# Attention and feed-forward kernel on one core: w_in's split moved from ScalarE and VectorE to VectorE and GpSimd, constant products at the start, a new order

## The chip, the core and the metric

The kernel runs on one core of one Trainium2 chip. The core has a matrix engine (TensorE, PE in the profile), three engines that work on rows of data (VectorE, DVE; ScalarE, ACT; GpSimd, POOL) and a queue engine that only starts transfers (SyncE, SP). Every engine works through its own list of instructions in order. SBUF is the working memory of 128 partitions; PSUM is the small memory that products are added up in. The metric is the device time of one execution in microseconds.

## What is computed

Eight batches of twelve heads of attention over 448 positions of 64 values, where the softmax is replaced by a sigmoid, and behind it a feed-forward layer whose activation is ELU. Heads are put side by side, so that a token has 768 values.

```python
# q, k, v: (8, 12, 448, 64); w_in: (768, 2048); w_out: (2048, 768)
scores = scale * np.matmul(q, k.transpose(0, 1, 3, 2)) - np.log(S)
attn = 1.0 / (1.0 + np.exp(-scores))
attn_out = np.matmul(attn, v)
x = attn_out.transpose(0, 2, 1, 3).reshape(B * S, H * D)
h = x @ w_in
g = np.where(h > 0.0, h, np.exp(np.minimum(h, 0.0)) - 1.0)
out = g @ w_out
```

## The kernel before

**Precision.** The products run in 16-bit floats, but the result is to have more than 16 bits give. So each operand is scaled by a power of two and split into a high part (the value rounded to f16) and a low part (the value minus its high part, in f16), and each product is made of three: high by high, high by low, low by high. For w_in and w_out that split is preceded by a reading of 64-bit words from the two matrices, which are taken apart, and by the search for the scale. The first six of the 48 pairs of heads are multiplied in f32 instead (`EXACT`).

**Stages.** A pair of heads goes through loads, maxima, scales, split, transposes, scores (`Pair.scores`, `psc`), sigmoid (`soften`, `sg`), its own split, and the product with v (`Pair.values`, `pav`), which gives rows of `xh`. A layer b then goes through the 16 columns blocks f of w_in (`Expert.products`, tile `ph`), exponential, missing part, ELU (`e`), the split into `g`, and the second product with w_out (`moe2_tile`, `po`).

**What sets the order.** Everything up to the start of layer 1 is written out by hand in the string `ORDER`: 890 letters, each of which takes one step of a generator (the dictionary `streams` names them). A step issues its instructions on whatever engines it uses, so the string sets the order on every engine at once; there is no scheduler behind it (`manual_schedule`). From layer 1 on the order is that of a plain loop over layers, with `fill` putting pieces of `moe2` between pieces of attention.

**How w_in gets ready** (letters i, A to G; 16 steps each, one for a block of 768 by 128 values). The letter i loads a block's words. A takes the magnitudes' upper field (`field`) and its last bits (`last_bits`), two instructions of ScalarE, into one of five staging places in `g` (`staged(f)`). B puts them together on VectorE (`magnitudes`). C adds up the magnitudes by six products with a constant (`si`). D takes the greatest sum on VectorE and makes the scale `ws`, the last instruction of it on GpSimd (`twice_inverse`). E puts the signs back, in place, on VectorE (`signed`). F makes the high part: ScalarE multiplies the staged f32 block by the scale and writes f16 (`w_in_high`, L291). G makes the low part: VectorE multiplies the staged block by the scale and subtracts the high part (`w_in_low`, helper `low`, L189). A staging place is free for block f+5 when G of block f has read it.

**How a pair of the first six gets turned** (letters d, e). TensorE transposes q and k into PSUM (`transposes`, tile `pt`), and VectorE copies the 896 columns into SBUF (`copied`, L492).

The lines of the steps of w_in on which the change works:

```python
# w_in_high
nc.scalar.mul(wi[:, 0, :, f * P : (f + 1) * P], staged(f), w_in_scale[f])
# w_in_low
d = wi[:, :, :, f * P : (f + 1) * P]
low(d[:, 1], staged(f), w_in_scale.pop(f), d[:, 0])
# twice_inverse, the last instruction of a scale
nc.gpsimd.tensor_scalar(dst, dst, 2 / least, None, op0=ALU.min)
```

Other letters that matter below: m is `Expert.products` of layer 0, R the rescaling of layer 0's `xh` to one scale (`rescale`, five multiplications on VectorE and then `greatest`, whose tile is `dg`); it needs the scales of all six pairs, which GpSimd carries on from pair to pair (`value_scale`, tile `xs`). The letter p is a piece of the second product, H to N are for w_out what A to G are for w_in.

Of the kernel before, what the change touches and what calls it, by code (L numbers as in the profile page):

```python
# [11 lines left out]
F32 = mybir.dt.float32  # L12
# [4 lines left out]
ALU = mybir.AluOpType  # L17
# [14 lines left out]


ORDER = (
    "iqviqviiiAAAadbceSTABCDEaSTFdbWBceCSSWDEAABGTTFCWWEGDAABSCiqvXFAATATAiiYYDGBECEaSSBFWbCD"
    "TTAAFAAdWWWcEDeGBGSCBSCEEqivFTXATASTiiiiqAAYDaWdbDGBYceWWCSSFFBDGEAATTTCBDEWCSSXAATTFEYD"
    "GWvBaYiiqdWCbWWGceFAAAADEBGSSCBDTFTAXAvadCbSToHEceSSYGRERYRDBRRiTHTAAWWWWCSTBIXFYSCEYEDR"
    "WTWTWWooHHqHvaRIauXHoHHFoHHqvYYIRRJJrJKKRDIsoKombJaaKxlHmoycbxHlffHHfsIcGsIygggsInHHIzGm"
    "JJmJJxlzyxzlLwyMMNNKmmmxFMMKNNKlzMMxlNyzMNwGyKtuoqvoffxMHlfHzHHmmgaNxMlaIgywNbJKyINMFzxm"
    "xMFlloNMHHJKowcwwwyygImmtzxHHlJNGKIyzxzzlfmffxMlqoHHJmwGwKyNywINvmzxzMlxMlfJwKwwgNymzxag"  # L40
    "ygaNzloHHMywINSSppppppppppTzJKwwgqovtpppppppppppppppppppkHHTIJKojSSbppppppppppppppppcaTT"
    "fffTHHaggIkJLMMNMNNMMNNMNgSSpbpWpppWpWppWTMMTNNKMMNNXYfgtqjvMMSSTNNcMYNMNffMgNMNkappWpWW"
    "WfppSTXTUgagVppppSSppfTTUUTpppppbUgYVqtvjkSSWcYVTTfUpWSpWpVaapppbppWpTfUUgVgSSppfUfXVVVg"
    "YcgkYWWTTUUSWWpptqvjSTSXRRVRRYVUVYRpWppTTTUUVSWWWaVSpppppppTXUTUfUffYYRVRVVgaWWWWppppfXY"
    "Ygggkjqjtv"
)


# [1 line left out]
def attention_ffn(  # L50
# [9 lines left out]
    nc = tc.nc  # L60
    B, H, S, D = q.shape
    DM, DF = w_in.shape
    P = 128
# [13 lines left out]
    WHOLE = FIRST + 2  # L77
    SP = 4
    SKEW = 2
    assert 2 * D == P and 2 * R == P and NK == NP  # L80

    const = ctx.enter_context(tc.tile_pool(name="const", bufs=1))
    sb = ctx.enter_context(tc.tile_pool(name="sb", bufs=1))
    ps = ctx.enter_context(tc.tile_pool(name="ps", bufs=1, space=PSUM))
# [7 lines left out]
    wi = const.tile([P, 2, NK, DF], F16, name="wi")  # L92
# [24 lines left out]
    w_in_words = []  # L117
    ones = const.tile([P, P], BF16, name="ones")
    nc.vector.memset(ones, 1.0)
    w_ones = const.tile([P, P], BF16, name="w_ones")  # L120
    nc.gpsimd.memset(w_ones, 2.0 ** (1 - WTOP))
    x_ones = const.tile([P, P], BF16, name="x_ones")
# [65 lines left out]
    def low(lo, src, s, hi):  # L188
        nc.vector.scalar_tensor_tensor(lo, src, s, hi, op0=ALU.mult, op1=ALU.subtract)  # L189
# [53 lines left out]
    def staged(f):  # L243
        return stage[:, (f + WT - NF) % WT].rearrange("p (c x) -> p c x", c=NK)
# [10 lines left out]
    w_in_sums, w_in_scale = {}, {}  # L255
# [32 lines left out]

    def w_in_high():
        for f in range(NF):  # L290
            nc.scalar.mul(wi[:, 0, :, f * P : (f + 1) * P], staged(f), w_in_scale[f])  # L291
            yield

    def w_in_low():
        for f in range(NF):
            d = wi[:, :, :, f * P : (f + 1) * P]
            low(d[:, 1], staged(f), w_in_scale.pop(f), d[:, 0])
            yield
    def w_in_ratios():
        nc.vector.tensor_reduce(wm[:, 0:1], wp, axis=AX.X, op=ALU.max)  # L300
# [30 lines left out]
    def w_out_fields():  # L331
        for i, f in each_w_out(NW):
            if f < NW - 1:
                t = wo[:, i, 2 * f + SKEW : 2 * f + SKEW + 2].rearrange("p f j c -> p f (j c)")
                t = t.bitcast(F32)
# [96 lines left out]
    class Preparation:  # L432
# [56 lines left out]

        def copied(self):  # L490
            qk = early[:, self.hp % 2]
            nc.vector.tensor_copy(qk, self.pt[:, : 2 * S])  # L492
            ready[self.n] = self.x_scale, 1 / math.sqrt(D), [qk], [self.rv]

        def natural(self, i):
# [606 lines left out]
    def outputs():  # L1102
# [6 lines left out]
        "t": pair_turned(), "u": whole_values(), "j": outputs(),  # L1109
        "A": w_in_fields(), "B": w_in_magnitudes(), "C": w_in_add(), "D": w_in_scales(),  # L1110
        "E": w_in_signs(), "F": w_in_high(), "G": w_in_low(),
        "H": w_out_fields(), "I": w_out_magnitudes(), "J": w_out_add(), "K": w_out_signs(),
        "L": w_out_scales(), "M": w_out_high(), "N": w_out_low(),
# [128 lines left out]
```

## Time and profile before

| | |
|---|---|
| three runs | 1170.59, 1171.21 and 1177.94 us, median 1171.21 us |
| the profiled execution | 1176.26 us, of which 1174.4 us are its span |
| mean granted TensorE clock | 0.993 of full speed |
| busy: PE, DVE, ACT, POOL | 1144.0, 728.6, 797.2, 182.4 us |
| chain that ended last | PE 85% of the span |

The span runs from the first instruction to the last; the 1.9 us around it belong to the execution's time. The profiled execution is 5.05 us (0.4%) above the median of the runs. A PE that is busy is not a PE at its peak, since matmuls overlap and their ends are modelled; what the table does show is that the other engines have room over the span as a whole. It says nothing of a stage, and the change lies in the first stage alone.

In the profile's views a row names a line of the kernel, an engine, an operation, the tiles (out<-in), the partitions by the elements of each, and how often. L189 is the helper `low`, L148 the last line of `twice_inverse`.

### The profile page before, as it was taken

Reading aid. Unit: us, or ns where it says so; the run is one execution under the profiler, and the core shown is the slowest. Engines: PE = TensorE matmul, PEld = TensorE weight load, DVE = VectorE, ACT = ScalarE, POOL = GpSimd, SP = SyncE. Lnnn points to the kernel's source line nnn. Section 1 sums busy time; section 2 is a strip of 40 time slices with the busy share of each in tenths; the row PEclk is TensorE's granted clock in tenths of the full one; section 3 lists DMA queues with packets and bytes.
Section 4 is the critical chain, followed back from the end, with each engine's and each line's share of the span. In section 5 each row is a group of like instructions: output and inputs, shape, how many; then the busy total and the mean of one; then the engine's idle time right before and its main releaser. Section 6 shows DMA issues by size and latency. Waiting matters only on the chain.

```text
span 1174.4 us, 23748 instructions
## 1 busy us (share of the span) xinstructions
PE 1144.0 (97%) x9662; PEld 635.1 (54%) x9662; DVE 728.6 (62%) x1346; ACT 797.2 (68%) x1184; POOL 182.4 (16%) x502
## 2 busy tenths in 40 slices
PE   5989899999999999999999999999999999999998
PEld 2335465555666555555666555555566555655565
DVE  5999868955666557855566556765476564853300
ACT  6989859777665678856766568857766567856500
POOL 2224113111121002201121111301022000300000
PEclk9999999999999999999999999999999999999999
DMA  9996544231242122503054131621234121310000
GB/s 261 254 259 181 123 127 95 58 85 41 55 102 62 41 41 58 125 24 80 8 103 102 24 66 28 122 55 42 48 73 94 45 51 38 72 37 1 1 27 27
DMA packets 219038, 92.12 MB, mean 78 GB/s; under 512 B 182448, under 2 KB 214832, under 8 KB 218928
## 3 DMA queue, kind: packets, MB, share of 16 engines
q1 hardware_dynamic: 217856, 90.28, 32.6%
q8 instruction: 75, 1.23, 0.4%
q10 hardware_dynamic: 1072, 0.33, 0.1%
q14 instruction: 35, 0.29, 0.1%
HBM read 60.29 MB, written 11.01 MB: 61 GB/s over the span
## 4 chain that ended last, share of the span: by engine, by line
PE 85%; ACT 2%; DVE 1%; DMA 1%; issue 0%; SPq 0%; POOL 0%; DVEq 0%; ACTq 0%; POOLq 0%
PE ph L728 33%; PE po L794 31%; PE pav L620 7%; PE psc L551 6%; PE po_r L794 5%; PE pscr L651 1%; DMA rv<-in_v_dram 1%; DMA ats<-in_moe_w_out_dram 1%; ACT wo L372 0%; DVE wo L189 0%; ACT wo L205 0%; ACT g L757 0%; ACT e L745 0%; ACT ats L210 0%; PE so L223 0%
## 5 line engine op out<-in xcount | busy, mean ns | idle before, releaser
L728 PE MATMUL ph<-xh,wi 128*128 128x448 f16 x2304 | 440.9, 353 | 0.4 <-DVE e L751 0.4
L794 PE MATMUL po<-wo,g 128*64 128x384 f16 (+1 forms) x4320 | 394.0, 327 | 0.0
L794 PEld LDWEIGHTS <-g 128*64 128x64 f16 (+1 forms) x4992 | 290.0, 109 | 161.7 <-issue 32.5
L728 PEld LDWEIGHTS <-wi 128*128 128x128 f16 x2304 | 224.0, 98 | 211.0 <-issue 5.0
L751 DVE SCALAR_TENSOR_TENSOR e<-ph,e 128x448 f32<-128x448 f32 x128 | 79.7, 623 | 183.7 <-ACT e L745 183.6
L189 DVE SCALAR_TENSOR_TENSOR ats<-sg,ats 128x896 f16<-128x896 f32 x120 | 127.6, 1089 | 104.4 <-ACT ats L588 104.4
L738 ACT ACTIVATE e<-ph,msc 128x448 f32<-128x448 f32 x128 | 80.7, 631 | 112.1 <-PE ph L728 94.5
L558 ACT ACTIVATE sg<-psc,bias,sc 128x896 f32<-128x896 f32 x126 | 134.1, 1094 | 6.4 <-PE psc L551 3.2
L627 ACT ACTIVATE xh<-pav,sc 128x448 f16<-128x448 f32 x48 | 30.4, 633 | 121.4 <-PE pav L620 119.7
L588 ACT ACTIVATE ats<-sg 128x896 f16<-128x896 f32 x120 | 109.5, 947 | 0.8 <-PE pav L620 0.2
L745 ACT ACTIVATE e<-e,msc 128x448 f32<-128x448 f32 x128 | 97.1, 760 | 4.3
L757 ACT ACTIVATE g<-e,rr 128x384 f16<-128x384 f32 (+1 forms) x192 | 95.3, 529 | 1.1 <-DVE e L751 0.7
L189 DVE SCALAR_TENSOR_TENSOR g<-e,rr,g 128x384 f16<-128x384 f32 (+1 forms) x192 | 94.7, 524 | 0.4
L551 PE MATMUL psc<-qk 64*128 64x448 f16 x756 | 87.0, 354 | 0.0
L148 POOL TENSOR_SCALAR sc<-sc 128x3 f32<-128x3 f32 (+1 forms) x48 | 13.5, 281 | 461.1 <-DVE pw L181 460.2
L620 PE MATMUL pav<-ats,vn 128*64 128x448 f16 x720 | 75.5, 353 | 0.0
L620 PEld LDWEIGHTS <-vn 128*64 128x64 f16 x880 | 49.8, 110 | 32.9 <-issue 2.6
L794 PE MATMUL po_r<-wo,g 128*64 128x384 f16 (+1 forms) x672 | 64.9, 326 | 0.0
L189 DVE SCALAR_TENSOR_TENSOR nat<-raw,sc,nat 128x384 f16<-128x384 f32 (+1 forms) x126 | 60.2, 525 | 1.1 <-ACT nat L503 0.3
L503 ACT ACTIVATE nat<-raw,sc 128x384 f16<-128x384 f32 (+1 forms) x126 | 59.8, 531 | 0.8 <-POOL sc L467 0.3
L189 DVE SCALAR_TENSOR_TENSOR xh<-pav,sc,xh 128x448 f16<-128x448 f32 x48 | 32.6, 680 | 39.9 <-ACT xh L627 39.9
L551 PEld LDWEIGHTS <-qk 64*128 64x128 f16 x756 | 30.2, 95 | 48.3 <-issue 29.7
(128 smaller groups left out, 968.9 us busy)
## 6 DMA issues: line engine op xcount, KB each, us to landing
wo<-in_moe_w_in_dram SPq DMA_DIRECT2D x14, 768.0 KB, 6.4
raw<-in_q_dram SPq DMA_DIRECT2D x48, 192.0 KB, 3.8
rv<-in_v_dram SPq DMA_DIRECT2D x48, 192.0 KB, 2.9
raw<-in_k_dram SPq DMA_DIRECT2D x47, 192.0 KB, 3.3
out_dram<-room SPq DMA_DIRECT2D x47, 192.0 KB, 2.1
wo<-in_moe_w_out_dram SPq DMA_DIRECT2D x9, 768.0 KB, 4.8
ats<-in_moe_w_out_dram SPq DMA_DIRECT2D x6, 768.0 KB, 4.7
rv<-in_v_dram SPq DMA_DIRECT2D x96, 32.0 KB, 2.5
```

What stands on the lines that cost most here:

```text
L189: nc.vector.scalar_tensor_tensor(lo, src, s, hi, op0=ALU.mult, op1=ALU.subtract)
L503: nc.scalar.mul(self.nat[:, 0, t : t + n], src, s)
L551: nc.tensor.matmul(psc[:, j, :S], kk[rows[j], o], qq[rows[j], :S], start=(n == 0), stop=(n == len(parts) - 1),)
L558: nc.scalar.activation(to, psc, AF.Sigmoid, bias=bias, scale=self.s_scale)
L588: nc.scalar.mul(hi, sg, 2.0**ATOP)
L620: nc.tensor.matmul(pav[rows[j], :S], vv[i][:, 2 * NC + j if g == NC else j * NC + g], sg[k][:, j], start=(g == 0 and n == 0), stop=(g == N ...
L728: nc.tensor.matmul(self.ph[f], wi[:, wj, c, f * P : (f + 1) * P], self.xh[c][:, xj], start=(n == 0), stop=(n == 3 * NK - 1),)
L738: nc.scalar.activation(self.e[f], self.ph[f], AF.Exp, scale=self.m[:, 0, f : f + 1])
L745: nc.scalar.activation(e, e, AF.Relu, bias=self.m[:, 1, f : f + 1], scale=self.m[:, 2, f : f + 1])
L751: nc.vector.scalar_tensor_tensor(e, self.ph.pop(f), 0.0, e, op0=ALU.max, op1=ALU.subtract)
L757: nc.scalar.mul(g[:, 0, f, o : o + n], self.e[f][:, i : i + n], self.xr)
L794: nc.tensor.matmul(po[r, :HM], tokens[:, r], wo[:, i, f, wj], start=(n == 0), stop=(n == 3 * NF - 1),)
```

## The change

Four things change.

1. TensorE gets 72 products of a constant matrix with itself (`ones`), 128 by 128, at the head of its list. Nothing reads their result.
2. For each of w_in's 16 blocks, F is now a multiplication of the staged f32 block by its scale, in place, on VectorE, and G is two instructions of GpSimd: a cast of the staged block to f16 (the high part) and a subtraction of that from the staged block (the low part). ScalarE's multiplication and VectorE's multiply-and-subtract are gone.
3. The copies of the six turned pairs go from VectorE to ScalarE.
4. `ORDER` is a new string of the same 890 letters, each as often as before.

```diff
-    "iqviqviiiAAAadbceSTABCDEaSTFdbWBceCSSWDEAABGTTFCWWEGDAABSCiqvXFAATATAiiYYDGBECEaSSBFWbCD"
+    "iqviiqviiAABadbCDEceSiSAABFCDEFaiTTAWAdSbcBeWSCTAATAATGAAWDBCEFWSSBEBGGTXTAAiAACCSEYDDDF"
...
+    IDLE = 72
...
     nc.vector.memset(ones, 1.0)
+    idle = ps.tile([P, 512], F32, tag="pav", name="idle")
+    for _ in range(IDLE):
+        nc.tensor.matmul(idle[:, :P], ones, ones, start=True, stop=True)
...
     def w_in_high():
         for f in range(NF):
-            nc.scalar.mul(wi[:, 0, :, f * P : (f + 1) * P], staged(f), w_in_scale[f])
+            t = staged(f)
+            nc.vector.tensor_scalar(t, t, w_in_scale[f], None, op0=ALU.mult)
             yield
 
     def w_in_low():
         for f in range(NF):
             d = wi[:, :, :, f * P : (f + 1) * P]
-            low(d[:, 1], staged(f), w_in_scale.pop(f), d[:, 0])
+            nc.gpsimd.tensor_copy(d[:, 0], staged(f))
+            nc.gpsimd.tensor_tensor(d[:, 1], staged(f), d[:, 0], op=ALU.subtract)
             yield
...
         def copied(self):
             qk = early[:, self.hp % 2]
-            nc.vector.tensor_copy(qk, self.pt[:, : 2 * S])
+            nc.scalar.copy(qk, self.pt[:, : 2 * S])
```

What the new string does to the lists of the engines is shown at three places. The first is GpSimd's list from the first pairs' scales on. Here `ws` is the scale of a block of w_in, `sc0_2`, `pw0_2` and `xs0` belong to pair 2 of layer 0, `wi` holds the split of w_in, and `g` is where its blocks are staged. Before:

```order
L423 TENSOR_SCALAR sc0_1_189<-xs0_141 128x1
L148 TENSOR_SCALAR ws_74<-ws_74 128x1 x4
L148 TENSOR_SCALAR sc0_2_348<-sc0_2_348 128x1
L184 TENSOR_SCALAR pw0_2_347<-pw0_2_347 128x1
L417 TENSOR_SCALAR xs0_141<-xs0_141,pw0_2_347 128x1
```

And now:

```order
L424 TENSOR_SCALAR xs0_226<-xs0_226,sc0_1_282 128x1
L429 TENSOR_SCALAR sc0_1_282<-xs0_226 128x1
L302 CAST wi_68<-g_70 128x6x128
L303 TENSOR_TENSOR wi_68<-g_70,wi_68 128x6x128
L152 TENSOR_SCALAR ws_74<-ws_74 128x1
```

GpSimd's list held only instructions on one column here; now the scale of block 2 (the L152) stands behind the cast and subtraction of block 0; two more pairs of cast and subtraction, of blocks 1 and 2, follow it, and only then the scales of blocks 3 to 5. Before, the scales of four blocks stood together (x4). Of the 16 casts and subtractions, 13 stand ahead of the scales of pair 5, which the rescaling of layer 0 needs; that is the second place, GpSimd's list ahead of them:

```order
L302 CAST wi_68<-g_70 128x6x128
L303 TENSOR_TENSOR wi_68<-g_70,wi_68 128x6x128
L152 TENSOR_SCALAR sc0_5_773<-sc0_5_773 128x1
L188 TENSOR_SCALAR pw0_5_772<-pw0_5_772 128x1
L423 TENSOR_SCALAR xs0_226<-xs0_226,pw0_5_772 128x1
```

Before, the same place held the scales of two blocks and no work on a block:

```order
L148 TENSOR_SCALAR ws_74<-ws_74 128x1 x2
L148 TENSOR_SCALAR sc0_5_662<-sc0_5_662 128x1
L184 TENSOR_SCALAR pw0_5_661<-pw0_5_661 128x1
L417 TENSOR_SCALAR xs0_141<-xs0_141,pw0_5_661 128x1
L418 TENSOR_SCALAR xs0_141<-xs0_141,sc0_5_662 128x1
```

What moved there is that the chain of scales from pair to pair runs behind the work on w_in. The third place is VectorE's list at the start. Before, behind three constants:

```order
L196 TENSOR_REDUCE mx0_0_121<-rv0_93 128x4
L178 TENSOR_REDUCE al_135<-pr_131 128x1
L144 TENSOR_SCALAR sc0_0_134<-al_135 128x1
L181 TENSOR_SCALAR pw0_0_133<-al_135 128x1
L492 COPY g_70<-pt0_0_123 128x896
L214 SCALAR_TENSOR_TENSOR g_70<-g_70,wo_69 128x768
```

And now:

```order
L218 SCALAR_TENSOR_TENSOR g_70<-g_70,wo_69 128x768
L200 TENSOR_REDUCE mx0_0_194<-rv0_166 128x4
L283 TENSOR_REDUCE alw_213<-si0_206 128x1
L148 TENSOR_SCALAR ws_74<-alw_213 128x1
L234 SCALAR_TENSOR_TENSOR g_70<-wo_69,g_70 128x768
L182 TENSOR_REDUCE al_220<-pr_204 128x1
```

The magnitudes of w_in's block 0 (L214, now L218) moved from behind pair 0's maxima, scales and copy to the head of the list, and the copy is gone from it. On SyncE's list the load of a third block of w_in moved ahead of q of pair 1; the loads ahead of that are the same. From layer 1 on no instruction moved.

More of the change, by code (lines that the diff above doesn't have):

```diff
@@ L34 @@
 ORDER = (
-    "iqviqviiiAAAadbceSTABCDEaSTFdbWBceCSSWDEAABGTTFCWWEGDAABSCiqvXFAATATAiiYYDGBECEaSSBFWbCD"
[L36 to L45, printed above, removed]
+    "iqviiqviiAABadbCDEceSiSAABFCDEFaiTTAWAdSbcBeWSCTAATAATGAAWDBCEFWSSBEBGGTXTAAiAACCSEYDDDF"
+    "BEFBFqiviWWTGGGAAadCqiWWCbEBDYDEceSSCAXTATYvBDFaEYFiiiqGGdWSCWbceASTABDAWCTWSATAXTSEDFEB"
+    "YFYCESGGATTAAvioiqBFaDBWdWWWbCceSCDEFDFSvGGGAHXTATSTYBEaWdWbCcYEeAHqoSSTTHWHWIITXARRYRBo"
+    "voSSTTHHHHCDaREYRRaIIWWWWXbcDYRYRJJJJKKRrRqoHHfffsIKvaKsgasgFoooougGmJmmxHlHxyIlyqtvHHHH"
+    "xlbJKKsIInymJJcLzxlzzMfMffmxKNywKalMHNgNMmmMzxHggyFNwNmMxllMNauozyzHMNbyINxMHlzMwNcFItqm"
+    "JxlfmKwNywwwMMzNfgyJKgvoHHxlMommzIwyaNzxflHxHMlJKoyGGmmNwaMzxNIyHlHxMJwNyImxlzzlJKKwwyyz"
+    "zwwwmxloHHfbcgIppppppppppJKyztNwgfffSSoqpppppppppppppppkjvHHTTgggIJKaoppppppppabpppppppH"
+    "HkISSJLTTTMMNNMNMNMNMMNNMMNMcNNppppppppWWWpSWSTMXMSKNMfTTqjtNYgNMkNfffgggvMMpppppWWWWSSf"
+    "TXTUUNYagaVNYYVjqvtppppppSSbpppTTTUUWpSSWTTUpppcaaVVVpWSppppWpppkfUTffSSpbpUUXfVgggVVTTY"
+    "gcWWWWppSjtSqvpppppUUffXTTUTUSSYRRRVRgYYVagRVkVaTTpWWWWUUSpppppXTUfUfVVYYVVpWWWpWXppppgR"
+    "RgYYktqjjv"
 )
```

## The prediction

> **What bounds the kernel now.** I read first the busy rows of the page, then the three stretches that the change divides the span into, then what TensorE waits for.
>
> ```profile
> PE 1144.0 (97%) x9662; PEld 635.1 (54%) x9662; DVE 728.6 (62%) x1346; ACT 797.2 (68%) x1184; POOL 182.4 (16%) x502
> 0.00:84.47 84.47, 63.24 (x343) 26.49 (x344) 69.59 (x134) 67.20 (x84) 19.99 (x55) 0.94 0.95 260
> 84.47:231.50 147.03, 141.32 (x1168) 75.38 (x1166) 123.38 (x222) 123.89 (x187) 38.62 (x84) 0.98 0.51 121
> 231.50:1174.40 942.90, 939.42 (x8154) 533.22 (x8153) 535.60 (x992) 606.11 (x914) 123.75 (x363) 1.00 0.25 55
> PE pt L485 <- DMA raw<-in_q_dram: 7.6, 1, 7.6
> PE si L223 <- DVE g L214: 5.2, 6, 3.1
> PE so L223 <- DVE wo L214: 3.0, 2, 2.8
> PE psc L551 <- DVE g L492: 2.0, 2, 1.5
> ```
>
> In the rows of stretches the columns behind the length are PE, weight loads, DVE, ACT and POOL, then granted clock, DMA share and GB/s. The cuts are the first matmul of layer 0 (84.47) and of layer 1 (231.50). Behind 231.50 no instruction moves, so 942.90 us stay. Between the cuts PE is busy for 141.32 of 147.03 us. In front of 84.47 it is idle for 21.2 us: there it waits, mostly for DVE. So the question is when the first matmul of layer 0 can run, and then whether PE stays as full as it was.
>
> It runs when the rescaling is through, whose last step is `dg` on DVE. DVE's groups between its first real instruction (8.97) and `dg`, by shape, those that the change touches or the sum uses, and `dg` itself from the timeline:
>
> ```profile
> L214 DVE SCALAR_TENSOR_TENSOR g<-g,wo 128x768 uint32<-128x768 uint32 x14 | 13.3, 952 | 0.0
> L230 DVE SCALAR_TENSOR_TENSOR g<-wo,g 128x768 uint32<-128x768 uint32 x14 | 13.2, 951 | 0.1
> L189 DVE SCALAR_TENSOR_TENSOR wi<-g,ws,wi 128x768 f16<-128x768 f32 x11 | 11.1, 1009 | 0.0
> L492 DVE COPY g<-pt 128x896 f32<-128x896 f32 x6 | 6.5, 1080 | 0.0
> L279 DVE TENSOR_REDUCE alw<-si 128x1 f32<-128x128 f32 x15 | 4.2, 283 | 1.8 <-PE si L223 1.8
> L144 DVE TENSOR_SCALAR ws<-alw 128x1 uint32<-128x1 uint32 x15 | 2.3, 154 | 0.5
> L674 DVE TENSOR_SCALAR xh<-xh,rr 128x896 f16<-128x896 f16 x5 | 2.1, 446 | 0.0
> L214 DVE SCALAR_TENSOR_TENSOR g<-g 128x768 uint32<-128x768 uint32 x2 | 1.9, 954 | 0.2 <-ACT g L210 0.2
> L230 DVE SCALAR_TENSOR_TENSOR g<-g 128x768 uint32<-128x768 uint32 x2 | 1.9, 953 | 0.0
> L214 DVE SCALAR_TENSOR_TENSOR wo<-wo 128x768 uint32<-128x768 uint32 x2 | 1.9, 953 | 0.0
> L214 DVE SCALAR_TENSOR_TENSOR wo<-wo,g 128x768 uint32<-128x768 uint32 x1 | 0.9, 949 | 0.0
> ...
> 83.74 0.29 DVE L153 TENSOR_SCALAR dg<-ident,rr 128x128 bf16<-128x128 f32 x1
> ```
>
> The idle column is near nothing: DVE is what bounds this stage. The change takes work from it, and gives work to POOL, busy for 19.99 of 84.47 us.
>
> **The change part by part, in this stage.**
>
> *VectorE.* Eleven L189 on wi (11.1 us) and six copies L492 (6.5) leave, 17.6 us. In come 13 multiplications in place, one more L214 (0.95), one more L279 (0.28) and four one-column instructions like L144 (0.6), as the order counts them ahead of `dg`. The in-place multiplication, one input of 768 f32, has no row. It lies between L674 (446 ns for 896 f16) and L189 (1009 ns for 768 with two inputs). I take 0.61, for L674 does 896 elements in less than half the time of L189's 768, so one-input work in SBUF is fast, and f32 has twice its bytes: 13 x 0.61 = 7.9 us (ends 5.8 and 13.1). DVE's sum falls by 17.6 - 9.7 = 7.9 us (10.0 to 2.7).
>
> *The start.*
>
> ```profile
> 6.37 0.86 ACT L210 ACTIVATE wo<-wo 128x768 uint32<-128x768 uint16 x1
> 8.97 0.69 DVE L196 TENSOR_REDUCE mx<-rv 128x4 bf16<-128x512 f32 x1 [7.76 <-DMA rv<-in_v_dram]
> 7.62 1.73 PE L485 MATMUL pt<-ident,raw 128*128 128x128 f32 x7 [7.62 <-DMA raw<-in_q_dram]
> 13.18 0.82 PE L223 MATMUL si<-g,w_ones 128*128 128x128 bf16 x6
> 44.20 0.98 PE L485 MATMUL pt<-ident,raw 128*128 128x128 f32 x7
> ```
>
> DVE now begins with block 0's magnitudes, which need ACT's end at 7.23, not v's landing: 8.97 - 7.3 = 1.7 us earlier. The loads it needs keep their place on SP. The 72 constant products stand in PE's 7.6 us of waiting. Their like is si, six for 0.82 us at the start's slow rate: 72 / 6 x 0.82 = 9.8 us from 1.0, which ends at 10.8 and would hold the first transposes up by 3.2. If they speed up the clock half-way, they end near 7.6 and the transposes take 0.98 and not 1.73. I set the two against each other, at nothing (ends +3.2 and -1.5), since DVE has a block of its own to do by then.
>
> *ScalarE.* It loses 11 multiplications of 0.93 here and gains six copies.
>
> ```profile
> L291 ACT ACTIVATE wi<-g,ws 128x768 f16<-128x768 f32 x16 | 14.6, 927 | 0.8 <-POOL ws L148 0.8
> L558 ACT ACTIVATE sg<-psc,bias 128x896 f32<-128x896 f32 x18 | 17.9, 1007 | 4.4 <-PE psc L551 4.3
> ```
>
> L558 is of the copy's shape, from PSUM: 6 x 1.0 = 6.0 against 10.2, so 4.2 us less on an engine that was busy for 67.20 of 84.47. It costs nothing, and gains nothing either while DVE or POOL is later.
>
> *GpSimd, alone.* Thirteen casts and subtractions stand ahead of pair 5's scales, which the rescaling needs. Their price has no row either; the nearest:
>
> ```profile
> masks.py:197 POOL MEMSET ident<- 128x128 f32 x1 | 0.2, 205 | 0.0
> L87 POOL MEMSET bias<- 128x1 f32 x1 | 0.1, 99 | 0.3 <-POOLq L1226 0.3
> masks.py:199 POOL TENSOR_SCALAR_AFFINE_SELECT ident<-ident 128x128 f32<-128x128 f32 x1 | 0.3, 294 | 0.1
> ```
>
> Writing 127 more elements takes 106 ns, 0.83 ns each; the select, which reads too, 195 more than one element, 1.53 each. So 768 elements take 0.74 to 1.27 us with one input. The subtraction reads two: from no more than that to twice the upper end, 0.74 to 2.44. I take 0.9 and 1.6, 2.5 us a block, in the middle of 1.5 and 3.7. Thirteen are 32.5 us (19 to 48), and with the 20 that POOL has it would still end ahead of DVE, if the two did not meet.
>
> The Trainium skill (GPSIMD Engine Reference, 3.1) gives some 2.6 cycles for an element of a two-input operation, 4497 ns for 2048 of f32; in proportion that is an estimate of 1.69 us for 768, so 2.6 a block, and 1.3 us more in all. No run here has shown it.
>
> *GpSimd and VectorE together.* They do meet. Rows of DVE and POOL from one timeline, and one group:
>
> ```profile
> 32.52 0.21 POOL L148 TENSOR_SCALAR ws<-ws 128x1 f32<-128x1 f32 x1 [4.87 <-DVE ws L144]
> 34.97 0.96 DVE L230 SCALAR_TENSOR_TENSOR g<-wo,g 128x768 uint32<-128x768 uint32 x1
> 35.03 0.96 POOL L148 TENSOR_SCALAR sc<-sc 128x1 f32<-128x1 f32 x1 [2.30 <-DVE pw L181]
> 36.24 1.08 DVE L492 COPY g<-pt 128x896 f32<-128x896 f32 x1
> 36.27 0.28 POOL L417 TENSOR_SCALAR xs<-xs,pw 128x1 f32<-128x1 f32 x1
> 96.93 0.50 POOL L704 TENSOR_SCALAR msc<-ws,xs 128x4 f32<-128x4 f32 x2
> 97.16 0.68 DVE L189 SCALAR_TENSOR_TENSOR nat<-raw,sc,nat 128x384 f16<-128x384 f32 x1 [0.35 <-ACT nat L503]
> L189 DVE SCALAR_TENSOR_TENSOR nat<-raw,sc,nat 128x384 f16<-128x384 f32 x84 | 51.6, 614 | 1.1 <-ACT nat L503 0.3
> ```
>
> An instruction of POOL on one column takes 0.21 us alone, but 0.96 when DVE starts one with two inputs in SBUF just ahead: it ends at 35.99, right behind DVE's 35.93. Beside DVE's copy from PSUM it is not held up. And the other way round, L189 on nat takes 0.68 and not 0.61 where POOL was at work as it began. So the two exclude each other where DVE reads two inputs from SBUF. In this stage those are 20 L214 (19.0 us), 16 L230 (15.1); I count the in-place multiplications (7.9) and L674 (2.1) with them: 44.1. With POOL's 32.5 that makes 76.6 us which can't overlap; DVE's other work, some 23, lies beside POOL's. Twenty-six hand-overs at about 0.15 (the 0.06 between 35.93 and 35.99, and part of the 0.21 that POOL needs for a single column) add 3.9: 80.5. From 7.3 on, `dg` comes at 87.8, not 83.7: 4.1 us later.
>
> The Trainium skill (SBUF — State Buffer, Who interferes with whom) has it as a lock: whichever comes first holds the shared pair of ports for the whole instruction, and the other waits. By that rule the 76.6 stand; the rows above agree as to POOL's wait, and with 0.07 us as to DVE's.
>
> *Behind the first matmul of layer 0.* DVE sheds the other five L189 (5.0) and gains three multiplications (1.8), three blocks on POOL come in at 2.5 each; PE waited for DVE there for little more than 3 us (so, above). I set this to nothing, from -3 (that wait goes) to +5 (two blocks held against DVE).
>
> **The sum.** 1176.26 for the profiled execution, + 4.1. It stands 5.05 us above the median, so the forecast is made against 1171.21: 1171.2 + 4 = 1175 us. About 1%, 11.7 us, is what a measurement of this kernel can tell from no change; this lies within it.
>
> **The rivals.**
>
> *VectorE isn't held up by GpSimd* (it runs on while GpSimd works into its gaps). For it speaks that the only row of a held DVE shows 0.07 us, and that POOL's 52 us fit into 84; against it, that POOL is held for the whole of DVE's instruction. Then DVE's sum decides: -7.9 and -1.7 for the start, 1171.2 - 9.6 = 1162 us (1155 to 1168, with the ends of the multiplication and the start). It ends under 1159.5 if PE's wait on `so` goes too.
>
> *GpSimd becomes the bound* (the other side). At 3.7 us a block POOL's part is 48.1, with 44.1 and 3.9 it is 96.1, `dg` at 103.4, and 1171.2 + 19.7 would be 1191; at 3.3 it is 1186. It decides from 3.1 us a block on, where 13 x 0.6 = 7.8 more than mine take the time past 1% over. For it speaks that the scales of blocks 2 to 5, which DVE waits for, stand behind casts in POOL's list; against it, that 3.1 is nearer the select's rate than the write's for both inputs. I put it at 1187.
>
> *The multiplication in place isn't fast.* At 1.01 each, as L189, 13 x 0.4 = 5.2 more on the same shared time: 1180 us. Then the change does not do what it says for VectorE. L674's 446 speaks against it.
>
> **How the numbers follow.** Forecast 0.43, VectorE not held 0.30, GpSimd the bound 0.20, the slow multiplication 0.07. Of the second about half lies under 1159.5: faster 0.16. Of the third most lies over 1182.9, and a little of the first and the last: slower 0.22; same 0.62. The range goes from 1158 (most of the second case) to 1189 (most of the third).
>
> **What would show it.** The cast and subtraction near 0.9 and 1.6 us, longer where DVE's two-input instructions run; L218 and L234 (the old L214 and L230) above 0.95 us where POOL came first; the multiplication near 0.61; DVE's first instruction near 7.3; PE's transposes at 0.98 from the start; the first matmul of layer 0 near 88 and of layer 1 near 235. If L218 keeps its 0.95 throughout and the first matmul of layer 0 comes near 75, VectorE isn't held, and I was wrong by about 13 us. If DVE's longest wait is for POOL's `ws`, GpSimd is the bound.

## The result

| | before | changed |
|---|---|---|
| median of the runs of one chip | 1171.35 us (4 runs, 1170.59 to 1177.94) | 1186.08 us (4 runs, 1184.92 to 1186.52) |
| profiled execution | 1176.26 us, span 1174.4 | 1186.52 us, span 1184.7 |
| first matmul of layer 0 | 84.47 | 97.93 |
| first matmul of layer 1 | 231.50 | 241.18 |

The ratio of the medians is 1.0112, with an interval of 1.0074 to 1.0149: the change costs 1.1%, 14.7 us. In the two profiled executions it is 10.3 us, since that of before lies 5 us above its median.

The busy times of the page of the changed kernel, over the whole span:

```profile
PE 1151.4 (97%) x9734; PEld 642.0 (54%) x9734; DVE 740.6 (63%) x1340; ACT 789.4 (67%) x1174; POOL 236.2 (20%) x534
```

Its three stretches, cut as those of before (columns: length, then PE, weight loads, DVE, ACT, POOL, granted clock, DMA share, GB/s):

```profile
0.00:97.93 97.93, 72.61 (x418) 32.89 (x419) 82.04 (x137) 66.01 (x83) 67.15 (x90) 0.88 0.85 228
97.93:241.18 143.25, 139.06 (x1166) 75.68 (x1164) 124.39 (x216) 117.46 (x177) 46.29 (x81) 0.99 0.50 121
241.18:1184.70 943.52, 939.77 (x8154) 533.43 (x8153) 534.20 (x989) 605.89 (x914) 122.74 (x363) 1.00 0.25 56
```

The loss lies ahead of layer 0 (+13.5 us); 3.8 come back between layers 0 and 1 in these two executions, and behind that nothing moves (943.52 for 942.90). VectorE is busy for 82.04 us ahead of layer 0 and not 69.59, though its own work there became less. Its groups by shape up to `dg`, and GpSimd's two new ones (L218, L234 and L193 are the old L214, L230 and L189; L296, L302 and L303 are the multiplication in place, the cast and the subtraction):

```profile
L218 DVE SCALAR_TENSOR_TENSOR g<-g,wo 128x768 uint32<-128x768 uint32 x14 | 18.5, 1321 | 8.2 <-ACT wo L214 8.2
L234 DVE SCALAR_TENSOR_TENSOR g<-wo,g 128x768 uint32<-128x768 uint32 x14 | 18.3, 1304 | 0.0
L296 DVE TENSOR_SCALAR g<-g,ws 128x768 f32<-128x768 f32 x13 | 11.8, 911 | 0.7 <-POOL ws L152 0.4
L200 DVE TENSOR_REDUCE mx<-rv 128x4 bf16<-128x512 f32 x7 | 4.8, 679 | 1.1 <-DMA rv<-in_v_dram 1.1
L218 DVE SCALAR_TENSOR_TENSOR wo<-wo 128x768 uint32<-128x768 uint32 x3 | 3.8, 1302 | 0.3 <-ACT wo L214 0.3
L218 DVE SCALAR_TENSOR_TENSOR g<-g 128x768 uint32<-128x768 uint32 x2 | 3.3, 1671 | 0.0
L234 DVE SCALAR_TENSOR_TENSOR g<-g 128x768 uint32<-128x768 uint32 x2 | 3.0, 1484 | 0.0
L218 DVE SCALAR_TENSOR_TENSOR wo<-wo,g 128x768 uint32<-128x768 uint32 x1 | 1.6, 1575 | 0.0
...
L303 POOL TENSOR_TENSOR wi<-g,wi 128x768 f16<-128x768 f32 x13 | 26.7, 2052 | 1.1
L302 POOL CAST wi<-g 128x768 f16<-128x768 f32 x13 | 16.6, 1277 | 1.3 <-DVE g L296 1.0
```

The same instructions took 0.95 us before. The excess of L218 is 14 x 0.37 + 3 x 0.35 + 2 x 0.72 + 0.62 = 8.3 us, of L234 14 x 0.35 + 2 x 0.53 = 6.0, of L296 over its 0.61 alone 13 x 0.30 = 3.9: VectorE was held for some 18.2 us (18.3 in the expectations below). One place of the timelines shows it, GpSimd's rows first, then VectorE's:

```profile
20.40 0.83 POOL L302 CAST wi<-g 128x768 f16<-128x768 f32 x1
21.31 1.64 POOL L303 TENSOR_TENSOR wi<-g,wi 128x768 f16<-128x768 f32 x1
23.90 1.42 POOL L302 CAST wi<-g 128x768 f16<-128x768 f32 x1
25.40 1.83 POOL L303 TENSOR_TENSOR wi<-g,wi 128x768 f16<-128x768 f32 x1
...
21.70 2.06 DVE L218 SCALAR_TENSOR_TENSOR g<-g,wo 128x768 uint32<-128x768 uint32 x1 [0.96 <-ACT wo L214]
23.68 0.94 DVE L234 SCALAR_TENSOR_TENSOR g<-wo,g 128x768 uint32<-128x768 uint32 x1
24.74 0.99 DVE L296 TENSOR_SCALAR g<-g,ws 128x768 f32<-128x768 f32 x1
25.65 2.39 DVE L218 SCALAR_TENSOR_TENSOR g<-g 128x768 uint32<-128x768 uint32 x1
```

The first cast and subtraction run alone: 0.83 and 1.64 us. L218 starts 0.39 us behind the subtraction and ends 0.81 us behind its end (21.31 + 1.64 = 22.95; 21.70 + 2.06 = 23.76): of its own 0.95 us nearly all came when GpSimd was through. Next the cast at 23.90, started behind L234, ends 0.70 us after L234 does, and L296 starts into that cast and takes 0.99 and not 0.61.

The last part of the stage: GpSimd's last pair of the thirteen, VectorE's wait for the scales behind it, `dg`, and the first matmul of layer 0.

```profile
80.73 2.24 POOL L303 TENSOR_TENSOR wi<-g,wi 128x768 f16<-128x768 f32 x1
...
84.71 0.23 DVE L675 TENSOR_SCALAR rr<-xs 128x6 f32<-128x6 f32 x1 [0.92 <-POOL xs L424]
96.06 0.29 DVE L157 TENSOR_SCALAR dg<-ident,rr 128x128 bf16<-128x128 f32 x1
...
97.93 1.36 PE L734 MATMUL ph<-xh,wi 128*128 128x448 f16 x5
```

From 20.4 to 85.0 GpSimd and VectorE hold each other up (VectorE is busy for 60.6 of these 64.6 us, GpSimd for 57.3); behind that VectorE has another 11 us of its own list up to `dg`.

### The profile page after: what moved, and what is told of

The parts are those of the page before. It is cut to its first block, busy times and chain, and to the rows that moved or that the text cites. A ratio compares the mean times of both kernels' runs of the same rounds, so it can differ in the third digit from the quotient of the medians.

```text
span 1184.7 us, 23898 instructions
## 1 busy us (share of the span) xinstructions
PE 1151.4 (97%) x9734; PEld 642.0 (54%) x9734; DVE 740.6 (63%) x1340; ACT 789.4 (67%) x1174; POOL 236.2 (20%) x534
## 4 chain that ended last, share of the span: by engine, by line
PE 87%; DVE 4%; ACT 2%; DMA 2%; POOL 2%; issue 1%; SPq 1%; ACTq 0%; DVEq 0%; POOLq 0%
PE ph L734 36%; PE po L800 31%; PE pav L626 7%; PE psc L557 6%; PE po_r L800 5%; PE pscr L657 1%; DMA raw<-in_k_dram 1%; DVE g L218 1%; POOL wi L303 1%; DMA wo<-in_moe_w_out_dram 1%; ACT sg L564 1%; ACT wo L378 1%; DVE g L234 1%; DMA qk<-nat 0%; PE so L227 0%
## 5 line engine op out<-in xcount | busy, mean ns | idle before, releaser
L193 DVE SCALAR_TENSOR_TENSOR ats<-sg,ats 128x896 f16<-128x896 f32 x120 | 127.6, 1089 | 105.9 <-ACT ats L594 105.9
L152 POOL TENSOR_SCALAR sc<-sc 128x3 f32<-128x3 f32 (+1 forms) x48 | 13.7, 285 | 440.5 <-DVE pw L185 439.6
L193 DVE SCALAR_TENSOR_TENSOR g<-e,rr,g 128x384 f16<-128x384 f32 (+1 forms) x192 | 96.1, 531 | 0.6 <-ACT g L763 0.2
L193 DVE SCALAR_TENSOR_TENSOR nat<-raw,sc,nat 128x384 f16<-128x384 f32 (+1 forms) x126 | 61.1, 535 | 0.8
L193 DVE SCALAR_TENSOR_TENSOR xh<-pav,sc,xh 128x448 f16<-128x448 f32 x48 | 32.6, 679 | 39.7 <-ACT xh L633 39.7
```

## The experiments

The chip differs from batch to batch, so each run is given as a ratio to the kernel before on its own chip (medians of before: 1173.95, 1174.06 and 1172.99 us in the three batches). Theory 1: GpSimd's casts and subtractions hold VectorE, and that is the loss. Theory 2: the new order itself is the loss.

**The split as before, all else changed.**

```diff
-            nc.vector.tensor_scalar(t, t, w_in_scale[f], None, op0=ALU.mult)
+            nc.scalar.mul(wi[:, 0, :, f * P : (f + 1) * P], staged(f), w_in_scale[f])
...
-            nc.gpsimd.tensor_copy(d[:, 0], staged(f))
-            nc.gpsimd.tensor_tensor(d[:, 1], staged(f), d[:, 0], op=ALU.subtract)
+            low(d[:, 1], staged(f), w_in_scale.pop(f), d[:, 0])
```

> The changed kernel with the two parts of w_in made as before (ScalarE's multiplication, VectorE's L193 from the staged words); new order, constant products and ScalarE's copies stay. Theory 1 (GpSimd's casts and subtractions hold VectorE): L218 and L234 fall from 1.30 to 0.95 us, VectorE's work ahead of dg is 80.2 - 18.3 (held) - 7.9 + 13 x 1.01 = 67 us, the first matmul of layer 0 comes near 84 to 86 and not at 97.9, the time is 1168 to 1176. Theory 2 (the new order itself costs, because TensorE's list has other work ahead of the first layer): the first matmul of layer 0 stays behind 93, the time above 1180.

1181.34 us, 1.0059 (1.0043 to 1.0075), first matmul of layer 0 at 95.83. These are theory 2's numbers. The row of the stage, then three of its waits:

```profile
0.00:95.83 95.83, 69.62 (x419) 32.09 (x419) 68.72 (x137) 75.69 (x97) 27.23 (x64) 0.91 0.85 233
```

```profile
DVE al L182 <- PE pr L178: 9.8, 4, 5.7
PE pav L624 <- ACT sg L562: 6.4, 3, 3.4
PE psc L555 <- ACT sg L562: 4.8, 2, 4.6
```

VectorE is down to 68.72 us, and its two-input instructions are no longer held:

```profile
L218 DVE SCALAR_TENSOR_TENSOR g<-g,wo 128x768 uint32<-128x768 uint32 x14 | 13.4, 958 | 9.3 <-ACT wo L214 9.3
L234 DVE SCALAR_TENSOR_TENSOR g<-wo,g 128x768 uint32<-128x768 uint32 x14 | 13.3, 951 | 0.0
```

Yet the stage is nearly as late. Now VectorE waits for TensorE and TensorE for ScalarE's sigmoids, behind which both the copies and thirteen multiplications stand in ScalarE's list. That the load on ScalarE is the reason is read from these waits; it is not tested by itself. The edit took GpSimd's part away and put another load on ScalarE; what it shows for theory 2 holds only if a run that puts nothing in its place shows it too.

**GpSimd's split alone, in the kernel before.** The same edit the other way round, old order, no constant products, copies on VectorE.

> The kernel before with only the multiplication in place on VectorE and GpSimd's cast and subtraction; old order, no constant products, copies on VectorE. Theory 1: eleven blocks ahead of dg, held time 11/13 of 18.3 = 15.5 us, VectorE's own work 68.9 - 11.1 + 6.7 = 64.5, so dg near 95 and the time 8 to 12 us over before, 1179 to 1184. Theory 2: within 3 us of before, 1168 to 1175.

1193.89 us, 1.0168 (1.0147 to 1.0190): a loss without the new order, so theory 2 can't be all of it, and larger than either theory gave. `dg` comes at 95.67, near theory 1's 95, and the first matmul of layer 0 at 96.71; the rest of the loss lies behind it, where the stretch up to layer 1 grows from 147.03 to 152.89:

```profile
0.00:96.71 96.71, 66.56 (x343) 27.52 (x344) 77.98 (x136) 58.49 (x73) 56.78 (x77) 0.86 0.84 230
96.71:249.60 152.89, 141.77 (x1168) 75.44 (x1166) 126.51 (x220) 120.41 (x182) 53.31 (x94) 0.98 0.48 115
```

A second way of losing time shows here. ScalarE waits for the staging places that GpSimd's subtraction gives back, 15.0 us up to the first matmul of layer 0 against 8.1 in the changed kernel:

```profile
ACT g L205 <- POOL wi L299: 15.0, 7, 4.3
```

**Nothing of GpSimd's split, and nothing in its place.**

```diff
-            nc.vector.tensor_scalar(t, t, w_in_scale[f], None, op0=ALU.mult)
+            hi = wi[:, 0, :, f * P : (f + 1) * P]
+            nc.vector.tensor_scalar(hi, t, w_in_scale[f], None, op0=ALU.mult)
...
-            nc.gpsimd.tensor_copy(d[:, 0], staged(f))
-            nc.gpsimd.tensor_tensor(d[:, 1], staged(f), d[:, 0], op=ALU.subtract)
...
-                for wj, xj in ((0, 0), (0, 1), (1, 0)):
+                for wj, xj in ((0, 0), (0, 1), (0, 0)):
```

> The changed kernel with GpSimd's casts and subtractions taken away and nothing put on another engine: VectorE's multiplication writes the high part of w_in at once, in float16, instead of the scaled words in place; the low part is left out, and the products that read it read the high part, so that TensorE has the same work. Order, constant products and ScalarE's copies stay. Theory 1 (GpSimd's instructions hold VectorE's): L218 and L234 are back at 0.95, the 18.3 us of holding go, the first matmul of layer 0 comes at 80 to 86 and not at 97.9, and the time is 11 to 15 us below the changed kernel's, 1170 to 1175. Theory 2 (the new order's own lists): the first matmul of layer 0 stays behind 92 and the time above 1181.

1169.71 us, 0.9961 (0.9949 to 0.9972), first matmul of layer 0 at 84.93. This is theory 1's number: with the same order, the loss is gone, and the strong form of theory 2 falls. The run makes no low part of w_in at all, though, so it shows what GpSimd's work costs in this order, and not that another engine would do that work for nothing.

**The cast without the subtraction.** Only the second of GpSimd's lines is taken out, and the products changed as above.

> The changed kernel without GpSimd's subtraction: the multiplication in place and GpSimd's cast stay, the low part of w_in is left out, and the products that read it read the high part. Theory 1: the held time goes with GpSimd's time, 0.83 of 2.47 us a block, so 18.3 falls to about 6; the first matmul of layer 0 at 84 to 90, the time 7 to 12 us below the changed kernel's, 1174 to 1179. Theory 2: behind 92 and above 1181.

1170.45 us, 0.9971 (0.9960 to 0.9982), first matmul of layer 0 at 85.59: in this order the cast costs next to nothing, the subtraction behind it all. The time lies below theory 1's range of 1174 to 1179: a share by time was too much. With the cast alone, the span up to 85 us and VectorE's two groups; then the same span with neither:

```profile
0.00:85.00 85.00, 66.18 (x414) 30.47 (x415) 66.91 (x135) 64.73 (x81) 39.22 (x76) 0.94 0.96 263
```

```profile
L234 DVE SCALAR_TENSOR_TENSOR g<-wo,g 128x768 uint32<-128x768 uint32 x14 | 16.3, 1165 | 0.0
L218 DVE SCALAR_TENSOR_TENSOR g<-g,wo 128x768 uint32<-128x768 uint32 x14 | 14.3, 1021 | 7.3 <-ACT wo L214 7.3
```

```profile
0.00:85.00 85.00, 65.81 (x419) 30.50 (x420) 63.04 (x136) 65.41 (x83) 25.32 (x64) 0.96 0.95 263
```

The casts do hold VectorE (L234 1.165 us, L218 1.021, 0.95 without), for 14 x 0.07 + 14 x 0.21 + 13 x 0.10 = 5.2 us in all. But VectorE has that much to spare: without them it is idle for some 15 of the 78 us from 7.2 on. How full the shared access is can be added up from the timelines: between 20 and 82 us, VectorE's magnitudes, signs, multiplications in place, low parts of `xh` and rescaling, or anything of GpSimd, run (overlaps counted once) for 45.4 of 62 us with neither, 51.7 with the cast, 60.2 in the changed kernel. The last is full. That fits a threshold rather than a share, below which the holding falls into time that VectorE had to spare; these are three points, and no run looks for the place of a threshold.

**One load more.** The question that is left by the last two: why does a VectorE with 15 us to spare bring nothing below 84? To the kernel without GpSimd's split comes a load that nobody uses.

```diff
             nc.sync.dma_start(st, src[:, :, f * P : (f + 1) * P])
             w_in_words.append(words(st))
+            if f == 9:
+                spare = ats.rearrange("p a i j s -> p (a i j s)").bitcast(U64)
+                nc.sync.dma_start(spare, w_in[:P, : spare.shape[1]])
```

> The run without GpSimd's casts and subtractions (low part of w_in left out there, its products read the high part), plus one more load that nobody uses: 1.38 MB of w_in into space that is free at that time, issued on SyncE's queue right behind the load of block 9. Theory 3 (without GpSimd's part the loads set the first matmul of layer 0: the DMA engines are 98% busy up to 80 us and move 269 GB/s): 1.38 MB is 5.1 us, so the first matmul goes from 84.9 to about 90 and the time from 1169.7 to 1173.5 to 1176. If VectorE's own list sets it, whose busy time is 63 us of the 78: 86 or less, and 1171 or less.

1172.73 us, 0.9991 (0.9979 to 1.0004), first matmul of layer 0 at 88.42: 3.5 of the 5.1 us show up, and 0.30% (3.5 us) in the ratio. So the loads carry most of that end, not all of it. What holds the loads up is seen in the changed kernel. The stretch from 40 to 60 us, before and then changed:

```profile
40.00:60.00 20.00, 17.41 (x106) 6.87 (x102) 19.76 (x39) 19.25 (x25) 5.89 (x13) 1.00 0.98 279
```

```profile
40.00:60.00 20.00, 14.55 (x77) 5.68 (x77) 19.41 (x35) 14.25 (x19) 18.52 (x20) 0.83 0.70 194
```

And what SyncE's queue waited for with w_in's loads up to 98 us (us in all, times, longest), before and then changed:

```profile
SPq L251 <- DVE g L230: 3.8, 4, 1.5
```

```profile
SPq L255 <- DVE g L234: 22.9, 9, 6.1
```

A block's words can be loaded once VectorE has put the signs on the block that lay there before. In the changed kernel these signs come late, the queue stands for 22.9 us, and the DMA share falls from 0.98 to 0.70; without GpSimd's split it is 10.6 us and 0.99. The DMA engines' work in front of layer 0 is about the same in all: 0.95 x 84.47 = 80, 0.95 x 85 = 81, 0.85 x 97.93 = 83 us. What they lose by standing is not made up. That the signs are what the loads stand for is so in this order. With GpSimd's split in the old order (the run above with the split alone, and the one with the old `ORDER` below) the queue waits only 6.3 and 6.5 us for signs, but 13.1 and 13.8 us for the places of v, which TensorE gives back late; the first matmul of layer 0 is late there too.

**The subtraction on VectorE.** `nc.gpsimd.tensor_tensor` becomes `nc.vector.tensor_tensor`, the cast stays.

> The changed kernel with the subtraction on VectorE, the cast stays on GpSimd. GpSimd's time falls by 13 x 1.64 = 21.3 us, VectorE's rises by 13 x 0.95 = 12.4. Theory 1: what VectorE has to do then is 66.9 (run with the cast alone) + 12.4 = 79.3 of the 78 us it had, so the first matmul of layer 0 at 91 to 95, the time 1176 to 1181: a subtraction costs VectorE less when it makes it itself than when GpSimd makes it. Rival (GpSimd's part is free work taken off VectorE): later than the changed kernel's 97.9, above 1187.

1186.84 us, 1.0117 (1.0098 to 1.0136): the changed kernel's 1.0112, between the two expectations. VectorE is held less here (L218 0.951 us, L234 1.102), but VectorE makes 13 subtractions of 1.09 itself, the signs come as late (SyncE's queue waits 21.2 us for them), and the first matmul of layer 0 is at 101.29. In this order the subtraction costs the same off VectorE or on it. The shared access, counted as above, is in use for 54.0 of 62 us: not full, and the loss is the same, so a full access is not the only way to lose this time. A longer list of VectorE's own does it as well.

**The cast on ScalarE.** `nc.gpsimd.tensor_copy` becomes `nc.scalar.copy`, GpSimd subtracts.

> The changed kernel with the cast on ScalarE; GpSimd only subtracts. Theory 1 with the shared access full (one-input work of GpSimd counts as well): GpSimd's time falls by 13 x 0.83 = 10.8 us, the stretch from its first to its last block by as much at most, the first matmul of layer 0 at 87 to 91, the time 1175 to 1180, if ScalarE, with 13 x 0.93 = 12 us more on 66, keeps up. Rival (only the subtraction, with its two inputs, shuts VectorE out): 95 or later, 1183 or more.

1192.97 us, 1.0171 (1.0152 to 1.0190), first matmul at 103.65. The rival's number, but not for its reason:

```profile
POOL wi L303 <- ACT wi L302: 14.4, 7, 5.5
DVE g L218 <- ACT wo L214: 12.7, 6, 6.1
ACT wi L302 <- DVE g L296: 12.0, 7, 2.8
```

The cast, in ScalarE's list, waits for VectorE's multiplication, GpSimd for the cast, and VectorE for the fields that stand behind the cast. A new wait hides what was asked; whether a one-input instruction of GpSimd counts for less than a subtraction is answered by the run with the cast alone, not by this one.

**The other parts one by one.** The changed kernel with the old `ORDER`; the kernel before with only the new one; with only the copies on ScalarE; with only the 72 constant products; and the kernel before once more.

> The changed kernel with the order of before; everything else as changed. If the new order makes up for most of what GpSimd's part costs (old order and GpSimd's part alone: 1.68% over before): 1188 to 1196. If what made up for it are the copies on ScalarE and the constant products: 1183 to 1188, as the changed kernel.

1196.05 us, 1.0181 (1.0166 to 1.0197). That is the upper end of what was expected if the order matters. The new order makes up for some 8 us, less than half of the split's price, most of it behind the first matmul of layer 0 (99.18 to 251.93, 152.75 us there and not 143.25).

> The kernel before with only the new order. If the order is neutral by itself: 1171 to 1177. If it fits only GpSimd's part and the copies on ScalarE (theory 2 in its weaker form): 1178 to 1186, with the first matmul of layer 0 behind 88.

1191.58 us, 1.0149 (1.0135 to 1.0162), later than expected, with the first matmul of layer 0 at 105.97. With the old instructions VectorE gives the word slots back late in the new order, and the loads stand for 24.0 us, 12.8 of them at once (the same view of SyncE's queue):

```profile
SPq L251 <- DVE g L230: 24.0, 5, 12.8
```

> The kernel before with only the copies of the turned pairs on ScalarE. If VectorE bounds the stage, 6.5 us leave it and ScalarE goes from 66.5 to 72.5 of 84: the time falls by 3 to 6 us, to 1165 to 1168. Rival: the copies stand in ScalarE's list between fields and sigmoids on which VectorE and TensorE wait, and the time stays within 3 us of before.

1178.09 us, 1.0027 (1.0013 to 1.0040): no gain, as the rival has it, and a small loss, 3.2 us by the ratio and so just beyond the rival's 3. The first matmul of layer 0 comes at 88.50. VectorE sheds 6.5 us and waits for TensorE's products instead:

```profile
DVE alw L279 <- PE si L223: 5.3, 2, 4.4
```

Before, that wait was 1.8 us.

> The kernel before with only the 72 constant products. Both theories: the transposes of pair 0 at 0.98 to 1.04 us and not 1.73, and nothing in the time (1168 to 1173), since VectorE still waits for v until 8.97. A third theory (an earlier granted clock lasts): first matmul of layer 0 at 83 or less and 1167 or less.

1170.54 us, 0.9975 (0.9962 to 0.9987): a gain, the only one of a complete kernel here, and this version is ahead of both. The time lies within the 1168 to 1173 of the first two theories, which stood for no change; against before on its own chip it is 0.25% less. Pair 0's transposes take 1.07 us. The first matmul, at 82.87, is the third theory's, the time is not.

> The kernel before once more, for a second profile of it: the first, at 1176.3, lay 5 us over its median. If the stretches of half the clock behind the first matmul of layer 0 come and go from run to run: 140 to 144 us between the first matmuls of layers 0 and 1 and not 147.0, and 1170 to 1174 in all. If they belong to the kernel: 147 again.

1176.48 us, and 147.06 us between the first matmuls of layers 0 and 1: as the first profile, so the stretches did not go. Both profiled executions lie near the top of the runs of before (1170 to 1178 us), though, and whether a quicker one has the same stretches was not seen. The rows between those matmuls, here and with the constant products:

```profile
84.70:231.76 147.06, 141.88 (x1167) 75.51 (x1166) 123.01 (x222) 122.98 (x186) 36.09 (x84) 0.97 0.50 120
```

```profile
82.87:224.60 141.73, 138.31 (x1168) 74.49 (x1166) 123.34 (x222) 123.31 (x187) 38.18 (x84) 1.00 0.51 126
```

TensorE is busy for 3.6 us less at the same number of products, at a granted clock of 1.00 and not 0.97. That is not shown to be the constant products' doing, for two kernels without them have it too. The kernel before with only the copies moved, then with only the new order:

```profile
88.50:231.05 142.55, 139.09 (x1167) 74.55 (x1165) 123.02 (x222) 122.89 (x187) 38.24 (x84) 0.99 0.49 123
105.97:246.87 140.90, 137.63 (x1165) 75.42 (x1164) 120.87 (x216) 121.34 (x184) 36.77 (x75) 1.00 0.50 123
```

And with GpSimd's split in the old order the stretch is as long with the constant products (152.75 us, copies moved too) as without (152.89).

## Why the prediction came out as it did

The time lies in the range (1186.08 in 1158 to 1189), and the price of 1.1% just over the 1% that was called no change. It came out where the rival "GpSimd becomes the bound" was put, 1187, and not at 1175. The range was wide enough for three rivals, so lying in it says little for the sum. Nor was the rival right: its sign was to be a long wait of VectorE for the scales `ws`, and that wait is 0.4 us.

- *The prices of single instructions* were right: cast 0.83 us (0.9), subtraction 1.64 (1.6), 2.47 a block (2.5); multiplication in place 0.61 where nobody is in the way (0.61). In part this is luck: the first two were taken from the middle of ranges of 0.74 to 1.27 and 0.74 to 2.44, and 0.61 does not follow from its two rows. Twice L674's time for an element gives 0.76, and a forecast 2 us later. The Trainium skill (GPSIMD Engine Reference, 3.1) led to an estimate of 1.69 for the subtraction; the trace agrees with 1.64.
- *That the two engines exclude each other* was right, and in both directions. The rival "VectorE isn't held up" falls with L218's 1.32 us.
- *The sum of the shared time* failed, at the step "From 7.3 on, `dg` comes at 87.8". It let 80.5 us of shared work fill the stage from VectorE's first instruction on. GpSimd begins its first block at 20.40 (the first multiplication in place is through at 14.58, but the cast stands behind pair 1's scales in GpSimd's list), and has none of the thirteen after 82.97, so the work of both had to go through a middle of 65 us, which it filled; VectorE then had 11 us of its own left. `dg` came at 96.06. The term was 4.1 us and measured 12.3. Taken apart: the prediction had -1.7 for the start and -7.9 for VectorE's own work, so 13.7 for the meeting of the two engines. The profiles have -1.8 and -6.9 (VectorE is busy for 68.57 us up to `dg` before and 79.88 now, 18.2 of them held), and for the meeting 18.2 of holding and 2.8 more of idle time. The price at which the rival was to decide, 3.1 us a block alone, was not reached; with its waits a pair took 1.28 + 2.05 = 3.33, which by the rival's own sum gives the 1186 that came. But those waits are the holding over again, in GpSimd's list.
- *"DVE is what bounds this stage"* was half of it. VectorE had little idle time before (6.2 of 74.8 us up to `dg`), but the loads had little either: their share, 0.95, stood in the row that the prediction quotes. With 63.04 us of work and not 69.59, and held by nobody, VectorE brought nothing below 84 (run without GpSimd's split); in the new order a late VectorE costs because the loads wait for its signs, as the queue's waits have it; no run tests that by itself.
- *The start*: VectorE began at 7.21 (7.3 forecast). What that is worth no run prices by itself.
- *The constant products* were set at nothing. At the start that held, near the favourable end:

```profile
1.04 6.67 PE L123 MATMUL idle<-ones 128*128 128x128 bf16 x72 [1.04 <-DVE half L129]
7.56 1.04 PE L491 MATMUL pt<-ident,raw 128*128 128x128 f32 x7
```

  They end as q lands, and the transposes take 1.04 and not 1.73 us. But alone they gain 0.25%; in the traces the first matmul of layer 0 comes 1.6 to 1.8 us earlier.
- *ScalarE's copies* at no cost: alone they lose 0.27%, with longer waits of VectorE for others. In the changed kernel, where ScalarE sheds the multiplications, no run priced them by themselves.
- *Behind the first matmul of layer 0* nothing was forecast, from -3 to +5; it was 147.03 to 143.25, -3.8. What gave it stays open: the constant products alone have 141.73 there, the copies alone 142.55, the order alone 140.90, and the 147 of before comes from two executions near the top of its runs.
- *The new order* had no price of its own in the prediction. By itself it costs 1.5%, and with the split it saves some 0.7% (1.0181 to 1.0112). Neither can be read from a sum over instructions.
- *Smaller slips in the working*: VectorE's work beside GpSimd's is some 17 us and not 23, since the six copies leave (68.6 - 7.9 - 44.1); the first rival's terms give 1158 to 1170 and not 1155 to 1168. Neither moves the forecast.

The experiments leave open how much of the loss goes through VectorE's held instructions, and how much through the staging places that GpSimd gives back late, on which ScalarE waits (8.1 us in the changed kernel, though ScalarE is not full; 15.0 with the split alone in the old order). No run takes the hold away while GpSimd still subtracts. For the hold speaks its size, 18.2 us, against some 4 us that VectorE waited from 20 to 85 us for others. So that GpSimd's split costs the time is shown, that the hold is the largest part of it in the changed kernel is read from the trace.

## What to carry to other kernels

Work that goes from a full VectorE to an idle GpSimd isn't taken off VectorE where the two hold each other up: add up the shared time of both within the stretch in which GpSimd can have work at all, not over the stage. Here little was lost at 51.7 of 62 us and 13 us at 60.2. Before counting a relieved engine as a gain, look for a second one that is just as full; here it was the DMA column of the same row. An edit in hand-ordered lists is priced with its order: the split alone cost 1.7% in the old order, the order alone 1.5% with everything else as before, and the order with the old split, copies moved and constant products 0.6%.

## What was not expected of the hardware

- VectorE's multiplication with one f32 input in SBUF is held by GpSimd as well, 0.61 us alone and 0.91 in the mean of thirteen, while its reductions are not (L200 679 ns, 682 before). The Trainium skill (SBUF — State Buffer, Who interferes with whom) names `tensor_scalar` among the operations that can take the shared pair and says that `tensor_reduce` never contends on trn2; the trace agrees in both.
- 72 products that nobody reads, in a stretch where TensorE waits for a load anyway, go with transposes of 1.04 to 1.07 us behind them and not 1.73, and alone with 0.25% over the runs. The 5.3 us between the first matmuls of layers 0 and 1 (147.06 to 141.73) are not theirs as far as the runs show, since two kernels without them have 140.90 and 142.55 us there.
